# Moving one set of transposes and three load steps in a hand-ordered attention and gated-linear-unit kernel

## The chip, the cores and the metric

The kernel runs on one core of one Trainium2 chip. The metric is device time in microseconds of one execution. Three runs of the kernel before took 190.13 to 190.59 us; their median is 190.49 us.

A core has a matrix engine (PE, TensorE), a vector engine (DVE), a scalar engine (ACT) and a general engine (POOL), each with its own queue of instructions that is worked off in order, and a queue (SP) that issues DMAs and also works in order. An instruction that waits for a semaphore holds up everything behind it in its queue. PE writes into PSUM, which has eight banks here numbered 0 to 7; DVE and ACT read them; POOL and the DMAs work on SBUF alone.

## The reference

There are 8 batches, 8 heads, 576 positions and a head dimension of 64. First comes causal attention with a bias that is a running sum, then a gated linear unit over the 512 columns that the heads make together. Cut to what matters:

```python
scores = scale * np.matmul(q, k.transpose(0, 1, 3, 2))
bias = -(cum[:, :, :, None] - cum[:, :, None, :])        # cum = running sum of max(s, 0)
scores = np.where(causal, -1e9, scores + np.minimum(bias, 0.0))
attn = exp(scores - max); attn = attn / (attn.sum(-1) + 1e-9)
x = np.matmul(attn, v)                                   # heads side by side: (8, 576, 512)

gate_pre = sum over 5 taps of conv_w[k] * x shifted by 4 - k positions
out = (sigmoid(gate_pre) * (x @ w_val)) @ w_out
```

All inputs and the output are float32; the kernel works in bfloat16 between float32 sums.

## The kernel before

**Units of work.** Two heads of one batch are a pair. There are 32 pairs, `n` = 0 to 31, four to a batch: batch `b` = `n // 4`. A step is one small piece of work for one pair, one batch or one tile of output, and is written as a name with its indices, such as `s0.21`. For a batch, K and Q are loaded (`ld_q.b` brings heads 0 to 3 of both Q and K, `ld_k.b` heads 4 to 7 of both, each as two DMAs of 512 KB, line 436), cast to bfloat16 into a buffer `qkb` (`c_q.b`, `c_k.b`, line 374), and transposed on PE: `qq.b.0` transposes what `c_q.b` cast and `qq.b.1` what `c_k.b` cast. Each of the two sets is 32 transposes of half the array (line 630), which alternate between two banks. Each bank is then copied out into `QKT` (`qe.b.p`, `p` = 0 to 3; `qe.b.0` and `qe.b.1` belong to `qq.b.0`, the other two to `qq.b.1`; line 374, a helper that all plain copies share). V is loaded by blocks of 128 positions (`ld_v.b.i`, line 472) and multiplied by a weight on POOL (`vp.b.p`, line 475), which needs all five blocks.

For a pair there are three groups of score products (`s0.n`, `s1.n`, `s2.n`, PE, line 506, each into two banks), their exponentials (`e0.n`, `e1.n`, `e2.n`, ACT, line 557, into one of three buffers P), a causal mask on POOL (`mk.n`, line 580), the product with V (`av0.n` and `av.n` for the two heads, line 595), reciprocal and normalisation on DVE (`rec.n`, `nm.n`, lines 608 and 614) and a transpose back to columns (`xt.n`, line 627, copied by `xe.n`). The convolution has four tap steps (`t1.n` to `t4.n`, on DVE at lines 666 and 671 or on POOL at line 674, some with a product `p2.n` to `p4.n` made ahead on POOL), then a tanh (`th.n`, ACT, line 691), the product with `w_val` (`val`, line 704) and the gate (`glu`, DVE, line 713). Two batches `u` share nine output tiles: `out.u.i` (PE, line 724, four products of 128x512 into one bank), `oe.u.i` (a copy into one of six tiles `ot`) and `st.u.i` (the store, line 732).

**What sets the order.** Nothing is planned when the kernel is built. The table `ORDER` names every step once, and the loop at the end of `main_path` calls the steps in that order. What follows the name is the engine (S for SP, G for POOL, T for PE, A for ACT, V for DVE), then the banks or the buffer: `s0.21:T:0+1:0` puts scores into banks 0 and 1 and their exponentials into P buffer 0. The order of the table is the order of each engine's queue; how the steps of different engines stand to each other is left to the semaphores, which are set by what each step reads and writes. Steps of different engines that only swap places in the table change nothing.

Around the change, the rows of batch 6, the seventh, stand between those of pairs 17 to 20. The banks there are: `qq.6.1` 7 and 3, `qq.6.0` 2 and 5, `out.1.6` 6, `xt.17` 3, `s2.20` 0 and 1, `out.1.8` 2, `av0.19` with `av.19` 6 and 7, `out.1.5` 4, `s0.21` 0 and 1. The scores `s0.20` are in banks 5 and 6, and `xt.18` is in bank 4, where DVE's taps of pair 18 read it. The loop that turns the table into instructions is this:

```python
    for name, e, *slots in steps:                      # line 772
        f, *ix = name.split(".")
        ...
        does[f](engines[e], *ix)                       # line 785
```

The steps that the change touches are written by these functions:

```python
    def qk_T2(e, b, h):                                # qq, line 635
        for p in range(2):
            for j in range(8):
                for r in range(2):
                    half_T(row_bank(b, h, r)[:, p * 512 + j * 64:p * 512 + j * 64 + 64], qk_src(None, b, 2 * h + p, j), r)
```

Of the kernel before, what the change touches and what calls it, by code (L numbers as in the profile page):

```python
# [16 lines left out]
B, H, S, D = 8, 8, 576, 64  # L17
# [229 lines left out]
val.13.0:T:4 t1.16:V:2 e1.18:A s2.18:T:5+6 vp.5.2:G glu.13.0:V val.15.0:T:2 t3.16:V st.1.0:S e2.18:A val.13.1:T:4  # L247
val.15.1:T:0 vp.5.1:G ld_v.6.1:S glu.13.1:V th.15:A:4 t4.16:V s0.19:T:5+6:2 av0.18:T:3+4 e0.19:A vp.5.0:G glu.15.1:V
av.18:T glu.15.0:V ld_v.6.4:S s1.19:T:0+1 rec.18:V s2.19:T:5+6 e1.19:A nm.18:V out.1.4:T:2 vp.5.3:G t2.16:V e2.19:A
tt.6:T:3 ld_v.6.3:S c_q.6:G:0 xt.18:T:4 oe.1.4:V:1 av0.17:T:0+1 te.6:A ld_k.7:S:2 xe.18:V s0.20:T:5+6:1 av.17:T  # L250
t1.18:V:0 e0.20:A qq.6.1:T:7:3 mk.19:G rec.17:V nm.17:V qe.6.3:A mk.20:G out.1.6:T:6 qe.6.2:V ld_v.6.0:S xt.17:T:3
p2.18:G:1 s2.20:T:0+1 qq.6.0:T:2:5 t4.18:V oe.1.6:A:5 qe.6.0:A e2.20:A out.1.8:T:2 qe.6.1:A st.1.6:S xe.17:V c_q.7:G:2
t3.18:V av0.19:T:6+7 th.16:A:1 st.1.2:S av.19:T t1.17:V:1 out.1.5:T:4 rec.19:V t2.18:G nm.19:V oe.1.5:A:3
s0.21:T:0+1:0 t4.17:V e0.21:A s1.20:T:6+7 st.1.5:S xt.19:T:4 ld_v.6.2:S out.1.7:T:5 t2.17:V e1.20:A mk.21:G ld_t.7:S
xe.19:V s1.21:T:0+1 oe.1.8:A:0 s2.21:T:6+7 t3.17:V p3.19:G:0 e1.21:A val.16.0:T:2 t1.19:V:3 val.18.0:T:3 e2.21:A
p4.19:G:1 val.17.0:T:0 glu.16.0:V t2.19:V val.16.1:T:1 th.17:A:0 st.1.4:S s0.22:T:6+7:2 t3.19:G th.18:A:2 glu.17.0:V
# [584 lines left out]
```

## Time and profile before

| what | value |
|---|---|
| median of 3 runs | 190.49 us |
| the profiled execution | 189.88 us |
| its span, first to last instruction | 188.2 us |
| granted TensorE clock, mean | 0.991 |
| PE busy | 173.1 us, 92% of the span |
| ACT busy | 171.5 us, 91% |
| DVE busy | 164.8 us, 88% |
| POOL busy | 162.0 us, 86% |
| DMA, mean over the span | 215 GB/s |

The profiled execution's own time is 1.68 us longer than its span: that lies around the first and the last instruction. All times below are from the start of the span. "Busy" is the sum of the times at which an engine worked on something; since matmuls are pipelined, a busy PE isn't at its peak. A row of a timeline gives the start, the length, the engine, the line in the kernel, the operation with what it writes and reads, and how often it stands there in a row; in brackets stands the idle time of the engine ahead of it, with the engine and line that ended it. Rows that start before the one above has ended overlap, as the engines are pipelined. For DMAs the length is that of the issue on SP; the time until the data has landed is given apart.

### The profile page before, as it was taken

What the parts mean: (1) busy time and instruction counts of PE and PEld (TensorE: products, weight loads), DVE (VectorE), ACT (ScalarE), POOL (GpSimd) and SP (SyncE); (2) the same over time, 40 slices, a digit from 0 to 9 for tenths busy, and PEclk for the clock granted to TensorE, in tenths of its full rate; (3) what the DMA queues carried; (4) which work ended last, traced back from release to release, by engine and by line L of the source; (5) the groups of instructions that cost most, each with busy time, mean ns of one, the idle gap of its engine ahead of it and who ended that gap; (6) DMA issues with size and microseconds to landing.
All of it is one profiled execution on the core that took longest, in us unless ns stands there. A gap on an engine that the chain in (4) does not pass through costs nothing.

```text
span 188.2 us, 6675 instructions
## 1 busy us (share of the span) xinstructions
PE 173.1 (92%) x2719; PEld 114.6 (61%) x2735; DVE 164.8 (88%) x320; ACT 171.5 (91%) x233; POOL 162.0 (86%) x145
## 2 busy tenths in 40 slices
PE   6999797889999999999969997999999999999991
PEld 2557384377757666576846674487566865767660
DVE  4867779879998899998999998889999899999980
ACT  3599969999999989999999988999999999999871
POOL 5149899898999999999999999599989989699530
PEclk9999889999999999999999999999999999999999
DMA  5999999799799999999799998869950003403064
GB/s 181 249 287 279 237 294 206 186 353 325 158 301 351 395 267 232 271 339 252 268 197 250 357 275 254 250 160 259 168 189 4 3 2 115 167 5 115 2 223 174
DMA packets 62283, 40.46 MB, mean 215 GB/s; under 512 B 47333, under 2 KB 49381, under 8 KB 62250
## 3 DMA queue, kind: packets, MB, share of 16 engines
q1 hardware_dynamic: 61706, 39.49, 76.7%
q10 hardware_dynamic: 544, 0.52, 0.8%
q8 instruction: 22, 0.36, 0.8%
q14 instruction: 11, 0.09, 0.1%
HBM read 30.57 MB, written 9.44 MB: 213 GB/s over the span
## 4 chain that ended last, share of the span: by engine, by line
PE 63%; ACT 20%; DMA 5%; SPq 4%; issue 3%; DVE 3%; ACTq 0%; DVEq 0%
PE bank L704 15%; PE bank L724 14%; ACT P L557 13%; PE bank L595 12%; PE bank L506 9%; PE bank L627 4%; PE bank L630 4%; DMA qkf<-in_k_dram 3%; PE bank L621 2%; ACT QKT L374 2%; DMA first<-in_k_dram 2%; SPq L468 1%; PE bank L519 1%; ACT ot L374 1%; ACT th L691 1%
## 5 line engine op out<-in xcount | busy, mean ns | idle before, releaser
L557 ACT ACTIVATE P<-bank 128x1024 bf16<-128x1024 f32 x84 | 83.1, 1044 | 3.3 <-PE bank L506 2.2
L671 DVE SCALAR_TENSOR_TENSOR gp<-bank,cwr,gp 128x574 f32<-128x574 bf16 (+6 forms) x71 | 51.1, 742 | 0.3
L674 POOL TENSOR_TENSOR gp<-gp,pr 128x572 f32<-128x572 f32 (+6 forms) x37 | 46.1, 1250 | 4.8 <-DVE gp L671 2.7
L506 PE MATMUL bank<-QKT 64*128 64x128 bf16 (+4 forms) x592 | 38.2, 237 | 4.6 <-ACT P L557 2.7
L475 POOL TENSOR_TENSOR Vp<-vst,w 128x650 bf16<-128x650 f32 x32 | 40.5, 1288 | 0.2 <-ACT w L395 0.2
L704 PE MATMUL bank<-xT,wv 128*128 128x288 bf16 (+2 forms) x256 | 38.2, 286 | 0.9 <-DVE gp L671 0.5
L595 PEld LDWEIGHTS <-P 128*128 128x128 bf16 x960 | 33.6, 98 | 5.6 <-issue 1.9
L595 PE MATMUL bank<-Vp,P 128*128 128x65 bf16 x960 | 36.5, 194 | 0.4 <-POOL Vp L475 0.2
L724 PE MATMUL bank<-wo,glu 128*128 128x512 bf16 x128 | 34.6, 380 | 2.2 <-ACT QKT L374 1.1
L506 PEld LDWEIGHTS <-QKT 64*128 64x128 bf16 x592 | 19.2, 94 | 22.4 <-issue 16.8
L655 POOL TENSOR_TENSOR pr<-xT,cwr 128x572 f32<-128x572 bf16 (+6 forms) x29 | 29.7, 1031 | 2.0 <-DVE xT L374 0.9
L704 PEld LDWEIGHTS <-wv 128*128 128x128 bf16 x256 | 22.5, 98 | 9.9 <-issue 3.8
L713 DVE SCALAR_TENSOR_TENSOR glu<-th,bank 128x288 bf16<-128x288 f32 (+2 forms) x64 | 26.9, 445 | 1.7 <-ACT th L691 0.5
L580 POOL TENSOR_SCALAR_AFFINE_SELECT P<-P 128x1024 bf16<-128x1024 bf16 (+2 forms) x19 | 19.1, 1010 | 10.0 <-ACT P L557 10.0
L666 DVE SCALAR_TENSOR_TENSOR gp<-xT,cwr,bank 128x576 f32<-128x576 bf16 (+2 forms) x36 | 26.6, 743 | 1.2 <-ACT xT L374 0.2
L614 DVE TENSOR_TENSOR xn<-bank,recs 128x640 bf16<-128x640 f32 (+2 forms) x36 | 26.8, 745 | 0.7
L374 ACT COPY QKT<-bank 128x1024 bf16<-128x1024 bf16 (+1 forms) x21 | 20.9, 1024 | 2.5 <-PE bank L490 1.3
L691 ACT ACTIVATE th<-gp,cwr 128x576 f32<-128x576 f32 x28 | 21.8, 799 | 0.0
L724 PEld LDWEIGHTS <-glu 128*128 128x128 bf16 x144 | 12.3, 97 | 13.5 <-issue 2.8
L374 ACT COPY ot<-bank 128x512 f32<-128x512 f32 x29 | 17.2, 609 | 2.2 <-PE bank L724 2.1
L374 DVE COPY QKT<-bank 128x1024 bf16<-128x1024 bf16 (+1 forms) x15 | 14.5, 969 | 4.1 <-PE bank L630 1.9
L627 PE MATMUL bank<-ident,xn 128*128 128x128 bf16 x164 | 15.0, 220 | 0.9 <-ACT P L557 0.6
(66 smaller groups left out, 183.6 us busy)
## 6 DMA issues: line engine op xcount, KB each, us to landing
out_dram<-ot SPq DMA_DIRECT2D x36, 256.0 KB, 3.1
vst<-in_v_dram SPq DMA_DIRECT2D x28, 256.0 KB, 5.9
first<-in_q_dram SPq DMA_DIRECT2D x6, 512.0 KB, 6.0
first<-in_k_dram SPq DMA_DIRECT2D x6, 512.0 KB, 6.9
qkf<-in_q_dram SPq DMA_DIRECT2D x6, 512.0 KB, 6.4
qkf<-in_k_dram SPq DMA_DIRECT2D x6, 512.0 KB, 6.4
vst<-in_v_dram SPq DMA_DIRECT2D x15, 128.0 KB, 4.6
first<-in_q_dram SPq DMA_DIRECT2D x4, 256.0 KB, 4.0
```

The lines of the kernel that those rows point to most:

```text
L374: (act.copy if e is act else e.tensor_copy)(dst, src)
L475: e.tensor_tensor(Vps[b % 2][:, :, HP[p]], vslot(b)[:, :, HP[p]], w[:, :, b * 8 + 2 * p:b * 8 + 2 * p + 2].unsqueeze(3).to_broadcast([128, ...
L506: pe.matmul(ps[:, hh, c0:c0 + nq], QKTs[b % 2][r, 1, p, k0:k0 + 128], QKTs[b % 2][r, 0, p, q0:q0 + nq], **kw)
L557: act.activation(out=Pt(n)[:, :, step * 512:(step + 1) * 512], in_=pair((f"s{step}", n)), func=AF.Exp, scale=0.125)
L595: pe.matmul(ps[:, o:o + 65], lhsT, Vps[b % 2][:, kb, 2 * p + w, :], start=(kb == 0), stop=(kb == qb))
L614: vec.tensor_tensor(xns[b % 2][:, g, p * 128:(p + 1) * 128].rearrange("t g (w d) -> t w g d", w=2), ps[:, :, :, 0:64], recs[:, n, :, g].un ...
L655: pool.tensor_tensor(pr, xTs[b % 2][:, c, 4 + lo - m:4 + hi - m], r.to_broadcast([128, hi - lo]), ALU.mult)
L671: vec.scalar_tensor_tensor(gp[:, lo:hi], xps(n, *h)[:, lo - m:hi - m], r, gp[:, lo:hi], ALU.mult, ALU.add)
L674: pool.tensor_tensor(gp[:, lo:hi], gp[:, lo:hi], prs[at[f"p{m}", n, *h][0]][:, lo:hi], ALU.add)
L704: pe.matmul(ps, wv[:, dc, c * 128:(c + 1) * 128], xTs[b % 2][:, dc, 4 + lo:4 + hi], start=(dc == 0), stop=(dc == 3))
L713: vec.scalar_tensor_tensor(glu2[:, c, o + lo:o + hi], th[:, lo:hi], 1.0, ps, ALU.add, ALU.mult)
L724: pe.matmul(bank_of(u, i), glu2[:, c, i * 128:i * 128 + 128], wo[:, c, :], start=(c == 0), stop=(c == 3))
```

## The change

The same steps are called, on the same engines, with the same banks and buffers. In the table, `qq.6.0` moves up to stand behind `qq.6.1`; `e2.20` moves down behind `th.16`; and `ld_v.6.3`, `ld_k.7` and `ld_v.6.0` move down behind the stores `st.1.6` and `st.1.2`. Two of the lines of the table that are new (the second begins with the moved loads):

```diff
+qq.6.1:T:7:3 mk.19:G rec.17:V nm.17:V qq.6.0:T:2:5 qe.6.3:A mk.20:G out.1.6:T:6 qe.6.2:V qe.6.0:A xt.17:T:3 p2.18:G:1
+ld_v.6.3:S ld_k.7:S:2 ld_v.6.0:S av.19:T t1.17:V:1 e2.20:A out.1.5:T:4 rec.19:V t2.18:G nm.19:V oe.1.5:A:3
```

On PE, where `qq.6.1` (which reads `qkb1`) ends, the rows stand like this; + is the kernel after, - the kernel before, and a row names the semaphores it waits for by their engine:

```order
 L630 LDWEIGHTS qkb1_103
 L630 MATMUL bank_153<-ident_67,qkb1_103 128x64
-L724 LDWEIGHTS glu2_115
-L724 MATMUL bank_153<-wo_143,glu2_115 128x512 [waits Activation_49]
+L630 LDWEIGHTS qkb0_102 [waits Pool_49]
+L630 MATMUL bank_153<-ident_67,qkb0_102 128x64 [waits DVE_49]
+L630 LDWEIGHTS qkb0_102
+L630 MATMUL bank_153<-ident_67,qkb0_102 128x64 [waits Activation_49]
```

The first product of `out.1.6`, which waited for ACT there, now follows the 32 transposes of `qq.6.0` (which read `qkb0`); these stood behind `s2.20` before. On ACT, in the same place, with the copies of `qe.6` into `QKT0`, of `oe.1.6` into `ot5` and of `oe.1.5` into `ot3`, the exponentials `e0.20` and `e2.20` into `P1`, and the tanh `th.16` into `th1`:

```order
 L557 ACTIVATE P1_117<-bank_153 128x2x512
-L374 COPY QKT0_107<-bank_153 128x2x2x256
-L374 COPY ot5_133<-bank_153 128x512
-L374 COPY QKT0_107<-bank_153 128x2x2x256
-L557 ACTIVATE P1_117<-bank_153 128x2x512
+L374 COPY QKT0_107<-bank_153 128x2x2x256 x2
+L374 COPY ot5_133<-bank_153 128x512
 L374 COPY QKT0_107<-bank_153 128x2x2x256
 L691 ACTIVATE th1_124<-gp2_121,cwr_144 128x576
+L557 ACTIVATE P1_117<-bank_153 128x2x512
 L374 COPY ot3_131<-bank_153 128x512
```

`qe.6.3` and `qe.6.0` now stand together ahead of `oe.1.6`, and `e2.20` stands behind `qe.6.1` and `th.16`. On SP, with `ld_v` into `vst0`, the two DMAs of `ld_k.7` into `qkf0`, and the stores from `ot5` (`st.1.6`), `ot4` (`st.1.2`) and `ot3` (`st.1.5`):

```order
 L472 DMA vst0_92<-in_v_dram 64x8x64
+L732 DMA out_0_dram<-ot5_133 128x512
+L732 DMA out_0_dram<-ot4_132 128x512
 L472 DMA vst0_92<-in_v_dram 128x8x64
 L436 DMA qkf0_136<-in_q_dram 64x4x512
 L436 DMA qkf0_136<-in_k_dram 64x4x512
 L472 DMA vst0_92<-in_v_dram 128x8x64
-L732 DMA out_0_dram<-ot5_133 128x512
-L732 DMA out_0_dram<-ot4_132 128x512
 L732 DMA out_0_dram<-ot3_131 128x512
```

Four DMAs, the three load steps, now stand behind two stores, the first of which waits for `oe.1.6`. On DVE and POOL the order is the same in both kernels.

More of the change, by code (lines that the diff above doesn't have):

```diff
@@ L249 @@
 av.18:T glu.15.0:V ld_v.6.4:S s1.19:T:0+1 rec.18:V s2.19:T:5+6 e1.19:A nm.18:V out.1.4:T:2 vp.5.3:G t2.16:V e2.19:A
[L250 to L253, printed above, removed]
+tt.6:T:3 c_q.6:G:0 xt.18:T:4 oe.1.4:V:1 av0.17:T:0+1 te.6:A xe.18:V s0.20:T:5+6:1 av.17:T t1.18:V:0 e0.20:A
+qq.6.1:T:7:3 mk.19:G rec.17:V nm.17:V qq.6.0:T:2:5 qe.6.3:A mk.20:G out.1.6:T:6 qe.6.2:V qe.6.0:A xt.17:T:3 p2.18:G:1
+s2.20:T:0+1 t4.18:V oe.1.6:A:5 out.1.8:T:2 qe.6.1:A st.1.6:S xe.17:V c_q.7:G:2 t3.18:V av0.19:T:6+7 th.16:A:1 st.1.2:S
+ld_v.6.3:S ld_k.7:S:2 ld_v.6.0:S av.19:T t1.17:V:1 e2.20:A out.1.5:T:4 rec.19:V t2.18:G nm.19:V oe.1.5:A:3
 s0.21:T:0+1:0 t4.17:V e0.21:A s1.20:T:6+7 st.1.5:S xt.19:T:4 ld_v.6.2:S out.1.7:T:5 t2.17:V e1.20:A mk.21:G ld_t.7:S
```

## The prediction

> **What bounds the kernel now.** I read the page first. Its chain of the work that ended last is shared out by engine like this:
>
> ```profile
> PE 63%; ACT 20%; DMA 5%; SPq 4%; issue 3%; DVE 3%; ACTq 0%; DVEq 0%
> ```
>
> No single engine bounds the program: the end passes from PE to ACT and back. So I took the chain in order of time at the place of the change, between 112 and 120 us (start, length, what):
>
> ```profile
> 115.19 1.01 ACT QKT L374
> 116.24 1.02 PE bank L724 x4
> ```
>
> The first is `qe.6.0`, ACT's copy of the transposes out of PSUM; the second is `out.1.8`, a product that goes into the bank which that copy empties. The chain runs through the steps that the change moves, so time won or lost here counts. Next, PE alone in order of time (start, length, engine, line, what; in brackets its idle time before and who ended it):
>
> ```profile
> 112.14 0.64 PE L630 MATMUL bank<-ident,qkb 64*128 64x64 bf16 x32
> 112.82 1.02 PE L724 MATMUL bank<-wo,glu 128*128 128x512 bf16 x3
> 113.92 0.44 PE L627 MATMUL bank<-ident,xn 128*128 128x128 bf16 x5
> 114.29 0.39 PE L506 MATMUL bank<-QKT 64*128 64x320 bf16 x4
> 114.52 0.63 PE L630 MATMUL bank<-ident,qkb 64*128 64x64 bf16 x32
> 116.24 1.02 PE L724 MATMUL bank<-wo,glu 128*128 128x512 bf16 x4 [1.10 <-ACT QKT L374]
> 117.10 1.08 PE L595 MATMUL bank<-Vp,P 128*128 128x65 bf16 x30
> 118.02 1.03 PE L724 MATMUL bank<-wo,glu 128*128 128x512 bf16 x3
> 118.98 0.83 PE L506 MATMUL bank<-QKT 64*128 64x128 bf16 x12
> ```
>
> These are, in order, `qq.6.1`, `out.1.6`, `xt.17`, `s2.20`, `qq.6.0`, `out.1.8`, `av0.19` with `av.19`, `out.1.5`, and `s0.21` with `s1.20`. PE stands still for 1.10 us ahead of `out.1.8`. ACT in the same stretch:
>
> ```profile
> 111.75 1.02 ACT L557 ACTIVATE P<-bank 128x1024 bf16<-128x1024 f32 x1 [0.34 <-PE bank L506]
> 112.85 1.01 ACT L374 COPY QKT<-bank 128x1024 bf16<-128x1024 bf16 x1
> 113.88 0.59 ACT L374 COPY ot<-bank 128x512 f32<-128x512 f32 x1
> 115.18 1.01 ACT L374 COPY QKT<-bank 128x1024 bf16<-128x1024 bf16 x1 [0.71 <-PE bank L630]
> 116.09 1.03 ACT L557 ACTIVATE P<-bank 128x1024 bf16<-128x1024 f32 x1
> 117.00 1.02 ACT L374 COPY QKT<-bank 128x1024 bf16<-128x1024 bf16 x1
> 117.90 0.80 ACT L691 ACTIVATE th<-gp,cwr 128x576 f32<-128x576 f32 x1
> 119.08 0.58 ACT L374 COPY ot<-bank 128x512 f32<-128x512 f32 x1 [0.39 <-PE bank L724]
> 119.56 1.95 ACT L557 ACTIVATE P<-bank 128x1024 bf16<-128x1024 f32 x2
> ```
>
> These are `e0.20`, `qe.6.3`, `oe.1.6`, `qe.6.0`, `e2.20`, `qe.6.1`, `th.16`, `oe.1.5`, then `e0.21` and `e1.20`. ACT waits 0.71 us for `qq.6.0` and then 0.39 us for `out.1.5`, which is late because PE stood still for ACT: one loss, paid on both engines. Its small gap ahead of `oe.1.6` (113.88 against 112.85 + 0.91, the step from one full-width start to the next at 115.18 and 116.09) is 0.12. All of ACT's loss is therefore 0.71 + 0.39 + 0.12 = 1.22 us.
>
> **The change on PE and ACT.** Nothing is added or removed; instructions only change places. `qq.6.0` now follows `qq.6.1`. What it waits for: its data, cast on POOL by `c_q.6` (first row below), done at 110.08 + 1.89 = 111.97; bank 5, which `e0.20` empties at 112.77; bank 2, emptied earlier on DVE. POOL, with rows that are needed later:
>
> ```profile
> 110.08 1.89 POOL L374 CAST qkb<-first 128x2048 bf16<-128x2048 f32 x1
> ...
> 120.67 1.09 POOL L580 TENSOR_SCALAR_AFFINE_SELECT P<-P 128x1024 bf16<-128x1024 bf16 x1 [2.29 <-ACT P L557]
> ...
> 125.48 1.89 POOL L374 CAST qkb<-qkf 128x2048 bf16<-128x2048 f32 x1
> 127.33 1.40 POOL L674 TENSOR_TENSOR gp<-gp,pr 128x572 f32<-128x572 f32 x1
> ```
>
> So `qq.6.0` starts at 112.82, where `out.1.6` starts now after the same wait for `e0.20`. It delays what follows by about 0.57 us (0.63 less the overlap that pipelined matmuls have). PE then runs `out.1.6` at 113.39, `xt.17` about 0.9 later at 114.29, `s2.20` at 114.66 (113.92 to 114.29 is 0.37), and reaches `out.1.8` at 114.9 (114.29 to 114.52 is 0.23).
>
> ACT: `e0.20` and `qe.6.3` stay where they are. `qe.6.0` follows at 112.85 + 0.91 = 113.76; its transposes end by 113.45, so it doesn't wait, and it ends at 114.77, before PE asks for bank 2 at 114.9. The 1.10 us is gone. Then `oe.1.6` at 114.67 (`out.1.6` ended near 114.4), `qe.6.1` 0.48 later (119.08 to 119.56) at 115.15, `th.16` 0.90 later at 116.05, and `e2.20`, now behind these, at 116.73 (0.80 less 0.12 of overlap, as 117.00 + 1.02 against 117.90). It ends at 117.75, where it ends at 117.12 now. That is the one price on this path: `s0.21` needs banks 0 and 1 from `e2.20`.
>
> What is late next on PE: `av0.19` comes at 114.9 + 0.86 = 115.76; its bank 6 is free when `oe.1.6` ends, 115.26. `out.1.5` comes 0.92 later, at 116.68, and needs bank 4 from DVE's `t3.18`, the first of these rows:
>
> ```profile
> 115.53 0.80 DVE L671 SCALAR_TENSOR_TENSOR gp<-bank,cwr,gp 128x573 f32<-128x573 bf16 x1
> 116.25 0.80 DVE L666 SCALAR_TENSOR_TENSOR gp<-xT,cwr,bank 128x576 f32<-128x576 bf16 x1
> 118.29 0.22 DVE L608 RECIPROCAL recs<-bank 128x10 f32<-128x10 f32 x1 [1.24 <-PE bank L595]
> ```
>
> It ends at 116.33: in time by 0.35. `out.1.5` ends at about 117.7, and `s0.21` starts at 117.8 behind `e2.20` (118.98 now: 1.18 earlier). `oe.1.5` starts at about 117.8 (119.08 now), and `e0.21` near 118.3 (119.56 now): 1.2 to 1.3 earlier. DVE's `rec.19` waits 1.24 now; its predecessor ends at 117.05, so it too can come 1.24 earlier. POOL's `mk.21` waits 2.29 for `e0.21`, so POOL can follow with 1.1 to spare. I take 1.2, the loss of ACT taken away whole. The ends: 1.3 by the starts just worked out; 0.7 if neighbours on ACT don't overlap (five steps at about 0.1 more each).
>
> **Whether it lasts to the end.** After 119 the engines look like this (stretch, its length, then busy time of PE, PEld, DVE, ACT and POOL; clock; DMA share; GB/s):
>
> ```profile
> 114.00:119.00 5.00, 3.85 (x80) 2.60 (x82) 3.73 (x7) 3.98 (x5) 4.38 (x4) 1.00 1.01 321
> 119.00:147.00 28.00, 27.11 (x442) 18.47 (x444) 26.69 (x49) 27.58 (x35) 25.52 (x21) 1.00 0.60 155
> ```
>
> ACT is busy for 27.58 of 28 us, and all four are chained to each other. If all can start 1.2 earlier, all stay 1.2 earlier; only what doesn't move with them can take it back. That is the loads.
>
> **The change on SP.** The stores `st.1.6` and `st.1.2` now stand ahead of `ld_v.6.3`, `ld_k.7` (two DMAs) and `ld_v.6.0`. `st.1.6` waits for `oe.1.6`, so these four DMAs wait with it. SP now (the third row is `ld_v.6.0`, the fourth begins with `st.1.6`):
>
> ```profile
> 110.20 2.51 SPq L436 DMA_DIRECT2D qkf<-in_q_dram  x1
> 112.75 0.62 SPq L436 DMA_DIRECT2D qkf<-in_k_dram  x1
> 113.42 0.60 SPq L472 DMA_DIRECT2D vst<-in_v_dram  x1
> 114.49 5.53 SPq L732 DMA_DIRECT2D out_dram<-ot  x3
> ```
>
> After: `st.1.6` at 115.3, where `oe.1.6` ends, and then some 0.6 each: `st.1.2` 115.9, `ld_v.6.3` 116.5, `ld_k.7` 117.0 and 117.6, `ld_v.6.0` 118.2. The second half of `ld_k.7` is issued 4.9 us later than now. Time to landing of the K and Q loads between 100 and 135 us, and of the V load ahead of `ld_k.7`:
>
> ```profile
> DMA to landing us min/median/max: 5.4/6.4/7.5
> vst<-in_v_dram SPq DMA_DIRECT2D x1, 256.0 KB, 6.8
> ```
>
> So it lands between 117.6 + 5.4 = 123.0 and 117.6 + 7.5 = 125.1. By bytes: the two stores, `ld_v.6.3` and `ld_k.7` are 1.84 MB; at the 321 GB/s of the row above that is 5.7 us, with some 2 us ahead of the first arrival 123.0. Who waits: `c_k.7` on POOL, at 125.48 now and wanted at 124.28; behind it `t4.19` (127.33, to 128.73), and for that ACT's `th.19`:
>
> ```profile
> 129.37 0.78 ACT L691 ACTIVATE th<-gp,cwr 128x576 f32<-128x576 f32 x1
> ```
>
> `th.19` starts 0.64 after `t4.19` ends, so `c_k.7` may start as late as 124.9 at no cost. The middle of the landing range, 124.0, is hidden; its late end, 125.1, would cost 0.2. The V loads have `vp.6.2` behind `t4.19`, later still, and I cost them at nothing.
>
> The V load of 256 KB takes 6.8 us where K and Q loads of 512 KB take 6.4, so bytes alone don't tell when what stands behind a V load lands, and I keep the whole landing range. By the Trainium skill, DMA: Bandwidth & Descriptors, Specifications, a transfer needs pieces of at least 512 B for line rate; a V row here is 64 floats, 256 B, and the trace agrees. By the same section's ceiling of 435 GB/s the 1.84 MB would take 4.2 us, an estimate by which `ld_k.7` would land 1.5 us sooner and the sum would stay as it is.
>
> **The sum.** The profiled execution took 189.88 us, 0.61 under the median of the runs, 190.49. 189.88 - 1.2 = 188.7; on the scale of the median, 189.3. About 0.3% (0.57 us) is what a measurement of this kernel can tell from no change.
>
> **The rivals.**
> - *The gain is smaller* (0.7): ACT's neighbours don't overlap. 189.8. Against it: starts 0.91 apart at 115.18, 116.09 and 117.00.
> - *The K load takes the gain back.* For no change `c_k.7` would have to start at 124.9 + 1.2 = 126.1, 8.5 us after its issue. Beyond the longest landing above, but reached if the issue stalls for a second as at 110.20 (2.51 us). About 190.5.
> - *Slower, by the same load.* It decides from a landing of 126.7 on. With the stall of 110.20 whole (1.9 more) and the longest landing it comes at 117.6 + 1.9 + 7.5 = 127.0; then `t4.19` ends at 130.3 and `th.19` starts 1.0 later than now: 191.5. For it: the landing and the stall were both seen. Against it: after the change SP issues nothing between the load ahead of `st.1.6` and 115.3, so what was queued has time to drain.
> - *PE's clock falls.* Granted clock in 114 to 119 is 1.00, with 32 transposes and a pause of 1.10 in it. If it halved for 2 of these 5 us, 1.5 us of work would take 3: 189.3 + 1.5 = 190.8. By the Trainium skill, TensorE: Matmul & The Clock Gate, Part 4, transposes don't count as busy for the gate in the same way, and 64 now stand together; the trace shows no fall after 32.
>
> **How the numbers follow.** Forecast 0.60 (own range 188.9 to 189.7), smaller gain 0.10, taken back 0.15, slower by the load 0.13, clock 0.02. Faster is 0.60 + 0.10 = 0.70; same 0.15; slower 0.13 + 0.02 = 0.15. The range leaves out the two slower cases and a little of the forecast's low end: 188.8 to 190.8.
>
> **What would show it.** Right: 64 transposes in one piece from 112.8 to about 113.4; no idle time on PE ahead of `out.1.8`; `qe.6.3` and `qe.6.0` back to back; `e0.21` near 118.3; POOL's `c_k.7` near 124.3 with no wait for a DMA; the rest of the trace as now, 1.2 earlier. Wrong: idle time on POOL ahead of `c_k.7` that a DMA ends, and then on ACT ahead of `th.19`; or `s0.21` held up by `e2.20` past 118.5.

## The result and the profile after

The kernel after takes 188.82 us (median of 11 runs) against 190.49 us (median of 11 runs of the kernel before): a ratio of 0.9916, 95% interval 0.9891 to 0.9941. That is 1.67 us, with an interval of about 1.1 to 2.1 us. The profiled execution took 188.30 us, with a span of 186.5 us (188.2 before). The forecast was 189.3. How much of the difference lies at the place of the change, the traces tell.

The chain that ended last, by engine; before, PE's share was 63% and ACT's 20%, and DMA had 5% and SP's queue 4%. These shares change from execution to execution (a second one of the kernel after has PE 59%, ACT 14% and SP's queue 12%), so nothing below rests on them:

```profile
PE 72%; ACT 18%; DVE 4%; issue 3%; POOL 0%; ACTq 0%; POOLq 0%; DVEq 0%
```

PE in order of time, at the place of the change:

```profile
111.75 1.30 PE L630 MATMUL bank<-ident,qkb 64*128 64x64 bf16 x64
112.98 1.04 PE L724 MATMUL bank<-wo,glu 128*128 128x512 bf16 x4
113.86 0.44 PE L627 MATMUL bank<-ident,xn 128*128 128x128 bf16 x5
114.23 0.39 PE L506 MATMUL bank<-QKT 64*128 64x320 bf16 x4
114.56 1.04 PE L724 MATMUL bank<-wo,glu 128*128 128x512 bf16 x4
115.43 1.08 PE L595 MATMUL bank<-Vp,P 128*128 128x65 bf16 x30
116.34 1.03 PE L724 MATMUL bank<-wo,glu 128*128 128x512 bf16 x4
117.42 0.72 PE L506 MATMUL bank<-QKT 64*128 64x128 bf16 x12
```

The 64 transposes are one piece, and `out.1.8` (114.56) follows `s2.20` with no idle time, where 1.10 us stood before. ACT in the same stretch:

```profile
111.35 1.02 ACT L557 ACTIVATE P<-bank 128x1024 bf16<-128x1024 f32 x1 [0.34 <-PE bank L506]
112.45 1.93 ACT L374 COPY QKT<-bank 128x1024 bf16<-128x1024 bf16 x2
114.27 0.61 ACT L374 COPY ot<-bank 128x512 f32<-128x512 f32 x1
114.74 1.05 ACT L374 COPY QKT<-bank 128x1024 bf16<-128x1024 bf16 x1
115.65 0.81 ACT L691 ACTIVATE th<-gp,cwr 128x576 f32<-128x576 f32 x1
116.32 1.04 ACT L557 ACTIVATE P<-bank 128x1024 bf16<-128x1024 f32 x1
117.41 0.58 ACT L374 COPY ot<-bank 128x512 f32<-128x512 f32 x1
117.89 1.95 ACT L557 ACTIVATE P<-bank 128x1024 bf16<-128x1024 f32 x2
```

The idle times of 0.71 and 0.39 us are gone. `e0.20` (first row) starts at 111.35 and `e0.21` (last row) at 117.89: 6.54 us apart, against 111.75 and 119.56, 7.81, before. So the place of the change gives 1.27 us. The other 0.40 us of the two profiled executions lies ahead of `e0.20`, where the two programs are the same on every engine but SP.

From `e0.21` to the end of the span it is 188.2 - 119.56 = 68.64 us before and 186.5 - 117.89 = 68.61 after: nothing of the 1.27 is given back, as far as spans read to 0.1 us can tell. The moved loads on SP, then POOL, then the tanh `th.19` on ACT:

```profile
114.90 1.41 SPq L732 DMA_DIRECT2D out_dram<-ot  x2
116.36 0.43 SPq L472 DMA_DIRECT2D vst<-in_v_dram  x1
116.83 0.71 SPq L436 DMA_DIRECT2D qkf<-in_q_dram  x1
117.59 0.61 SPq L436 DMA_DIRECT2D qkf<-in_k_dram  x1
118.25 0.60 SPq L472 DMA_DIRECT2D vst<-in_v_dram  x1
```

```profile
118.99 1.09 POOL L580 TENSOR_SCALAR_AFFINE_SELECT P<-P 128x1024 bf16<-128x1024 bf16 x1 [1.01 <-ACT P L557]
...
124.04 1.89 POOL L374 CAST qkb<-qkf 128x2048 bf16<-128x2048 f32 x1 [0.18 <-DMA qkf<-in_k_dram]
125.89 1.40 POOL L674 TENSOR_TENSOR gp<-gp,pr 128x572 f32<-128x572 f32 x1
```

```profile
127.69 0.78 ACT L691 ACTIVATE th<-gp,cwr 128x576 f32<-128x576 f32 x1
```

POOL's cast `c_k.7` does wait for the K load, by 0.18 us. `t4.19` ends at 127.29 and `th.19` starts at 127.69, so the wait costs nothing, but the cover left (the time by which `t4.19` could still come later at no cost) is 0.40 us.

### The profile page after: what moved, and what is told of

Read it like the earlier page. It is cut to its first block, busy times and chain, and to the rows that moved or that the text cites. A ratio compares the mean times of both kernels' runs of the same rounds, so it can differ in the third digit from the quotient of the medians.

```text
span 186.5 us, 6691 instructions
## 1 busy us (share of the span) xinstructions
PE 173.7 (93%) x2735; PEld 114.3 (61%) x2735; DVE 165.3 (89%) x320; ACT 171.3 (92%) x233; POOL 162.1 (87%) x145
## 4 chain that ended last, share of the span: by engine, by line
PE 72%; ACT 18%; DVE 4%; issue 3%; POOL 0%; ACTq 0%; POOLq 0%; DVEq 0%
PE bank L704 15%; PE bank L724 15%; PE bank L595 13%; ACT P L557 13%; PE bank L506 11%; PE bank L621 6%; PE bank L627 4%; PE bank L630 3%; PE bank L490 2%; PE bank L519 1%; PE bank L481 1%; ACT ot L374 1%; DVE gp L666 1%; DVE gp L671 1%; ACT th L691 1%
## 5 line engine op out<-in xcount | busy, mean ns | idle before, releaser
L506 PE MATMUL bank<-QKT 64*128 64x128 bf16 (+4 forms) x592 | 38.1, 237 | 4.5 <-ACT P L557 2.5
L724 PE MATMUL bank<-wo,glu 128*128 128x512 bf16 x144 | 36.0, 380 | 0.0
L506 PEld LDWEIGHTS <-QKT 64*128 64x128 bf16 x592 | 19.3, 94 | 22.1 <-issue 16.4
```

Of the source, the lines that this page charges most:

```text
L506: pe.matmul(ps[:, hh, c0:c0 + nq], QKTs[b % 2][r, 1, p, k0:k0 + 128], QKTs[b % 2][r, 0, p, q0:q0 + nq], **kw)
L724: pe.matmul(bank_of(u, i), glu2[:, c, i * 128:i * 128 + 128], wo[:, c, :], start=(c == 0), stop=(c == 3))
```

## The experiments

Two intervals sort the executions. The first, from the start of `e0.20` to that of `e0.21` on ACT, is the place of the change; the second, from the start of `e0.21` to the end of the span, is the rest. The first two columns of the table are read off ACT's timeline of each profiled execution, and the others follow from them and the span. The ratio is the measured time against the kernel before on the same chip, with its 95% interval; it isn't the quotient of the two medians and can differ from it by 0.001. Only "between" and "rest" tell where time was won; each is read from one execution.

| kernel | e0.20 | e0.21 | between | rest | ratio |
|---|---|---|---|---|---|
| before | 111.75 | 119.56 | 7.81 | 68.64 | 1 |
| after | 111.35 | 117.89 | 6.54 | 68.61 | 0.9916 (0.9891 to 0.9941) |
| after, again | 112.36 | 119.11 | 6.75 | 68.59 | 0.9925 (0.9899 to 0.9951) |
| order on PE and ACT only | 112.37 | 118.91 | 6.54 | 68.59 | 0.9927 (0.9896 to 0.9957) |
| loads only | 112.62 | 120.43 | 7.81 | 68.67 | 1.0011 (0.9990 to 1.0033) |
| half way | 113.28 | 120.37 | 7.09 | 68.63 | 0.9967 (0.9943 to 0.9991) |
| exponential back | 111.87 | 118.46 | 6.59 | 68.64 | 0.9946 (0.9928 to 0.9964) |
| K load one later | 112.53 | 119.07 | 6.54 | 69.63 | 0.9961 (0.9936 to 0.9987) |
| K load much later | 111.68 | 118.22 | 6.54 | 70.38 | 1.0149 (1.0111 to 1.0186) |

**The changed kernel again**, without an edit.

> The changed kernel itself, once more beside the others. Theory (one stall taken off PE and ACT, 1.27 us by the two profiles between e0.20 and e0.21): e0.21 starts 6.5 us after e0.20 (before: 7.8), ratio about 0.992 to 0.994. The 0.40 us by which its first profile was already ahead at e0.20, where the two programs are still the same, is jitter: it should come out differently here.

The gain is 1.17 us by the medians (188.96 against 190.13) and 1.4 by the ratio, 0.9925. `e0.20` now comes at 112.36, later than in the trace of before: the 0.40 us ahead of it was jitter (a difference between executions that no edit makes), as expected. Over all traced executions here `e0.20` starts between 111.35 and 113.28, though the programs are the same up to 110 us on every engine but SP. "Between" is 0.21 longer than in the first execution: ACT's `oe.1.5` waited for PE. On PE the delay arises in `xt.17`, which took 0.66 us instead of 0.44; the trace names no cause.

```profile
118.63 0.58 ACT L374 COPY ot<-bank 128x512 f32<-128x512 f32 x1 [0.25 <-PE bank L595]
```

**The order on PE and ACT only.** Against the kernel after, on SP:

```diff
+ld_v.6.3:S
+ld_k.7:S:2
+ld_v.6.0:S
 st.1.6:S
 st.1.2:S
-ld_v.6.3:S
-ld_k.7:S:2
-ld_v.6.0:S
```

> Only the order on PE and ACT is changed; the three load steps stand where they stood before. Theory: the whole gain is in this part, e0.21 starts 6.5 us after e0.20 and the ratio is that of the full change within 0.002, or better by at most 0.001, since POOL's cast of the moved K load waited 0.18 us for its DMA in the full change and this was hidden. Rival (the loads moved behind the stores give a part of the gain, since the DMA engines are clear for the stores): slower than the full change by 0.002 or more.

188.98 us, ratio 0.9927; 6.54 us between. The whole gain is in this part. The rival, that the moved loads give a part of the gain, asked for a ratio worse by 0.002 or more, and it isn't. POOL's cast starts without a wait:

```profile
124.83 1.89 POOL L374 CAST qkb<-qkf 128x2048 bf16<-128x2048 f32 x1
```

**The loads only.** The three steps are moved as in the diff above with + and - exchanged, now against the kernel before.

> Only the three load steps are moved behind the two stores; PE and ACT keep the order of before. st.1.6 is then issued near 114.5 and the second half of the K load near 117; it lands near 123.4, when POOL wants it at 125.5. Theory: no change, ratio 0.998 to 1.002, e0.21 7.8 us after e0.20, no DMA wait ahead of POOL's cast. Rival (the loads give a part of the gain): ratio under 0.997.

190.39 against 190.13 us, ratio 1.0011 with 1 in its interval; 7.81 us between. PE and ACT wait as before, here PE ahead of `out.1.8`:

```profile
117.11 1.02 PE L724 MATMUL bank<-wo,glu 128*128 128x512 bf16 x4 [1.10 <-ACT QKT L374]
```

So the loads by themselves give nothing.

**Half way.** Against the kernel before, on PE; ACT and SP keep their order:

```diff
 qq.6.1:T:7:3
 out.1.6:T:6
+qq.6.0:T:2:5
 xt.17:T:3
 s2.20:T:0+1
-qq.6.0:T:2:5
 out.1.8:T:2
```

> Only the 32 transposes of qq.6.0 are moved, and only half the way: behind out.1.6, ahead of xt.17. ACT and SP keep their order. Theory by the starts of the trace: qq.6.0 ends near 114.4 instead of 115.15, so ACT's qe.6.0 follows oe.1.6 with no wait (0.71 won); PE still waits for qe.6.0 ahead of out.1.8, by about 0.5 instead of 1.10. e0.21 starts 7.0 us after e0.20, a gain of about 0.8 us, ratio 0.995 to 0.997. Rival (only the order of the copies on ACT matters): no change, since ACT's order is that of before.

189.74 us, ratio 0.9967; 7.09 us between, a gain of 0.72 where 0.8 was expected. ACT's copy `qe.6.0` no longer waits for the transposes, and PE's wait for the copy is cut to 0.39:

```profile
115.41 0.59 ACT L374 COPY ot<-bank 128x512 f32<-128x512 f32 x1
115.98 1.01 ACT L374 COPY QKT<-bank 128x1024 bf16<-128x1024 bf16 x1
```

```profile
117.05 1.02 PE L724 MATMUL bank<-wo,glu 128*128 128x512 bf16 x4 [0.39 <-ACT QKT L374]
```

So 0.72 of the 1.27 us comes from the place of the transposes on PE, with ACT's order as it was; the rival, that only the order on ACT matters, is out. PE still waits, as `qe.6.0` starts at 115.98, right behind `oe.1.6` and just after the transposes end at 115.95. The other 0.55 came only with the last step up on PE and ACT's new order together: no run parts these two.

**The exponential put back.** Against the kernel after, on ACT:

```diff
 qe.6.0:A
 oe.1.6:A:5
+e2.20:A
 qe.6.1:A
 th.16:A:1
-e2.20:A
 oe.1.5:A:3
```

> The changed kernel with the exponential e2.20 put back ahead of qe.6.1 and th.16, all else as changed. s0.21 is then free of e2.20 about 1.5 us sooner. Theory: ACT is full from e0.20 to e0.21 either way, so e0.21 keeps its start, 6.5 us after e0.20, within 0.15, and the time is that of the changed kernel within 0.002. Rival (e2.20 moved down is what won the time): e0.21 comes 0.5 us or more later than in the changed kernel.

188.87 us (188.96 and 188.82 for the kernel after), ratio 0.9946 against a median of before of 189.82 on this chip; 6.59 us between. `e2.20` stands here right behind `oe.1.6`, and `e0.21` comes no sooner:

```profile
115.51 1.02 ACT L557 ACTIVATE P<-bank 128x1024 bf16<-128x1024 f32 x1
...
118.46 1.96 ACT L557 ACTIVATE P<-bank 128x1024 bf16<-128x1024 f32 x2
```

The place of `e2.20` is neither the gain nor a price that the runs can tell: in this trace and in the first of the kernel after, ACT shows no idle time from `e0.20` to `e0.21`.

**The K load one DMA later.** Against the kernel after, on SP:

```diff
 ld_v.6.3:S
-ld_k.7:S:2
 ld_v.6.0:S
+ld_k.7:S:2
 st.1.5:S
```

> The changed kernel with both halves of ld_k.7 moved behind one more DMA only, the V load ld_v.6.0. Second half issued near 118.2 instead of 117.6, so that it lands 0.6 to 1.5 us later. In the changed kernel th.19 has 0.4 us of slack. Theory: th.19 starts 0.2 to 1.1 us later, ratio to before 0.994 to 0.999. Rival (there is cover left): as the changed kernel, 0.9925.

189.44 us, ratio 0.9961: about half of the gain is gone by the ratios, though their intervals overlap (0.9936 to 0.9987 here, 0.9899 to 0.9951 for the kernel after). The trace, of the longest of the twelve executions (190.46 us), shows where. POOL's cast, then ACT's `th.19`:

```profile
126.66 1.89 POOL L374 CAST qkb<-qkf 128x2048 bf16<-128x2048 f32 x1 [1.61 <-DMA qkf<-in_k_dram]
```

```profile
129.93 0.78 ACT L691 ACTIVATE th<-gp,cwr 128x576 f32<-128x576 f32 x1 [0.94 <-POOL gp L674]
```

`th.19` starts 10.86 us after `e0.21` instead of 9.80, and the rest is longer by as much, 69.63 against 68.61. In this execution SP issued the second half at 119.53, 0.46 us after `e0.21`; in the kernel after it did so 0.30 us ahead of `e0.21`. The load then took 7.0 us to land, where POOL's cast in the kernel after started 6.45 us after the issue: 0.76 us of the delay is the issue, and the rest the landing.

**The K load much later.** Against the kernel after, on SP:

```diff
 ld_v.6.3:S
-ld_k.7:S:2
 ld_v.6.0:S
 st.1.5:S
 ld_v.6.2:S
+ld_k.7:S:2
 ld_t.7:S
```

> The changed kernel with both halves of ld_k.7 moved two DMAs further down, behind st.1.5 and ld_v.6.2. Its second half is then issued near 119.8 (117.6 in the changed kernel), lands near 126.2, and POOL's cast starts near 126.3 instead of 124.0. Theory (the slack of th.19 behind t4.19 is 0.4 in the changed kernel's trace, and from there on ACT pays): th.19 starts 1.6 to 2.0 us later than in the changed kernel, the whole gain is lost, ratio to before 0.998 to 1.004. Rival (the load has cover to spare, or later stages take the delay up): the ratio stays at 0.993 or less.

Three DMAs, counting `ld_v.6.0`, now stand ahead of the load that stood behind them. The profiled execution is as expected. POOL's cast, and `th.19`:

```profile
126.47 1.89 POOL L374 CAST qkb<-qkf 128x2048 bf16<-128x2048 f32 x1 [2.28 <-PE bank L506]
```

```profile
129.75 0.78 ACT L691 ACTIVATE th<-gp,cwr 128x576 f32<-128x576 f32 x1 [1.60 <-POOL gp L674]
```

The releaser named in the first row had long been done; the cast waits for the K load, issued at 119.98 with 6.3 us to landing, which is 126.28. `th.19` comes 11.53 us after `e0.21` instead of 9.80, 1.73 later, and this execution took 190.29 us, a ratio of 1.0025. But the median of the six runs is 192.42 us, ratio 1.0149, which is over the expected 1.004: the other five took 191.75 to 193.36, and without the two longest the median is still 191.85. So four more executions of the same kernel were traced, numbered 2 to 5 here.

> The kernel with the late K load once more, to see what its slower executions are made of: its profiled execution lost 1.8 us behind e0.21, but its other runs were 1.5 to 3 us above that one. Theory (the time to landing differs from run to run, and past the slack each us of it is a us of the end): the K load lands later than 6.3 us after its issue whenever the span is longer than 188.6, POOL's cast and th.19 come later by as much, and span minus the start of th.19 stays at 58.8 within 0.3. Rival (the loss lies in a later stage, such as the loads behind the K load): span minus the start of th.19 grows.

> As for the second look at the late K load: one more execution, for the spread.

> The late K load once more, in search of one of its executions of 191.7 us and more, of which none is in a trace so far. Theory: as in the looks before, span minus the start of th.19 is 58.8 within 0.3, and what is longer lies between the issue of the K load and th.19. Rival: it lies before e0.20 or behind th.19.

> As for the fourth look at the late K load: one more execution, in search of a slower one; span minus the start of th.19 is 58.8 within 0.3.

Executions 2, 3 and 4 took 190.96, 190.64 and 191.08 us (the kernel before beside them: 190.13 in the median for 2 and 3, one run of 190.98 for 4 and 5), and span minus the start of `th.19` was 58.76, 58.83 and 58.83, as in the kernels before (58.83) and after (58.81). The expectation that a longer span goes with a longer landing didn't hold in execution 2: its load landed 6.2 us after the issue, no later than the 6.3 of the first, and its span was 0.6 us longer mainly because `e0.20` came 0.54 us later. Execution 5 is one of the long ones: 193.26 us. Its `th.19`, then PE behind it:

```profile
131.36 0.77 ACT L691 ACTIVATE th<-gp,cwr 128x576 f32<-128x576 f32 x1 [2.65 <-POOL gp L674]
```

```profile
132.67 0.39 PE L506 MATMUL bank<-QKT 64*128 64x64 bf16 x4 [2.47 <-DVE glu L713]
```

Two things add up. `th.19` comes 12.57 us after `e0.21`, 1.04 more than in the first execution: SP issued the second half of the load 2.46 us after `e0.21` (1.76 there), and it took 6.7 us to land (6.3 there). And span minus the start of `th.19` is 191.6 - 131.36 = 60.24, 1.4 more than anywhere else. The granted clock of PE (the third number from the end; 1.00 is full speed) fell there, by stretches of 2 us:

```profile
132.00:134.00 2.00, 1.17 (x9) 0.45 (x11) 1.83 (x4) 2.00 (x4) 2.00 (x3) 1.00 0.65 149
134.00:136.00 2.00, 2.00 (x39) 1.36 (x39) 2.00 (x4) 1.84 (x3) 2.00 (x2) 0.52 0.89 198
136.00:138.00 2.00, 2.00 (x27) 1.18 (x26) 1.69 (x3) 1.68 (x4) 2.00 (x3) 0.62 0.06 15
```

After PE had stood for 2.47 us its clock read 0.52 and 0.62 over these 4 us, which is 3.4 us at half. In execution 4, where PE stood for 1.62 us at the same place, it stayed at 1.00:

```profile
131.78 0.39 PE L506 MATMUL bank<-QKT 64*128 64x64 bf16 x4 [1.62 <-DVE glu L713]
```

```profile
134.00:136.00 2.00, 2.00 (x52) 1.48 (x45) 2.00 (x4) 2.00 (x4) 2.00 (x2) 1.00 0.45 96
```

The expectation for executions 4 and 5, that all of the extra time lies ahead of `th.19`, fell with execution 5: behind it lie 1.4 us, where the clock fell. That the idle time of PE made it fall is inferred from this one execution, and another fall warns against a simple rule: in seven of the thirteen traces the clock goes to 0.50 for 3.4 us near 22 us, in execution 5 too, and there no idle time of PE was over 0.63 us in the 8 us before. PE was merely thinly used, busy for 1.16 of 2 us:

```profile
20.00:22.00 2.00, 1.16 (x13) 0.70 (x13) 1.82 (x4) 2.00 (x5) 2.00 (x3) 0.86 0.87 200
22.00:24.00 2.00, 1.97 (x27) 0.85 (x28) 0.65 (x1) 2.00 (x3) 2.00 (x2) 0.50 0.96 263
```

The same program shows this early fall in executions 1 and 5 and not in 2, 3 and 4. That the other long executions are made like execution 5 isn't shown, since none of them is in a trace.

## Why the prediction was right

The time predicted was 189.3 us, with 188.9 to 189.7 as the forecast's own range, and 188.82 and 188.96 were measured. The direction and the mechanism held. The first median is 0.08 us below that own range and only 0.02 above the low end of the whole range, 188.8 to 190.8; that it stayed inside is luck, since its size holds some 0.4 us that the change didn't make.

- *The stall and its size.* "The loss of ACT taken away whole", 1.2 us, measured 1.27 between `e0.20` and `e0.21` (1.06 in the second execution). The rival of a smaller gain, 0.7, is out: the two copies in a row took 1.93 us, where one alone takes 1.01, so neighbours on ACT do overlap. The starts worked out on PE and ACT, shifted by the 0.40 us by which the execution was ahead, hold within 0.07 us: `out.1.8` worked out at 114.5 and measured at 114.56; `th.16` 115.65 and 115.65; `e2.20` 116.33 and 116.32; `e0.21` 117.9 and 117.89. What is late next on PE was named rightly too: bank 4 and bank 6 were free in time, and `s0.21` (117.42) follows the end of `e2.20` (117.36).
- *It lasts to the end.* The rest is 68.59 to 68.67 us in the seven executions of the table in which the K load was in time, that of before among them. Everything behind `e0.21` moved as one.
- *The loads.* The landing of `ld_k.7` was put at 123.0 to 125.1 and taken at the middle, 124.0, with no wait at the cast. What was off is the issue, not the landing: SP issued the second half at 117.59, which is 118.0 on the scale of the prediction and not 117.6, and the cast started 6.45 us later, near the median of 6.4 that was used. So the cast came 0.4 later than worked out, and it waited 0.18 us for the load, and 0.33 in the second execution. This is the one sign that came out wrong; the cover that was worked out for it took it up, with 0.40 us left, and 0.25 in the second execution. The K load one DMA later shows how near the edge it stood: there the rival "the K load takes the gain back" is half true. That the load held is therefore in part luck.
- *The rival on the clock.* In the changed kernel the clock stays at 1.00 with 64 transposes together, so they didn't lower it. Where it fell behind the change, in execution 5 of the late load, an idle time of PE stood ahead of the fall. By the Trainium skill, TensorE: Matmul & The Clock Gate, Part 1, the clock falls to half after an idle window of about 3.4 us. Execution 5 agrees on the half (0.52), but its idle time was shorter, 2.47 us, and the falls near 22 us came with none over 0.63.
- *The size of the median.* 1.67 us in the first comparison and 1.17 in the second. The traces explain 1.27 and 1.06 by the change; the first comparison's surplus is inside its interval, and its profiled execution had 0.40 of it ahead of the change.

## What to carry to other kernels

Where two engines each wait for the other within a microsecond, look for one work item that both waits share: moving 32 transposes up by three places, with the copy that follows them moved up on ACT, took away waits of 0.71 and 0.39 us on ACT and 1.10 us on PE, which were one loss of 1.27; the transposes moved up by two places alone gave 0.72. Before a load is moved down, follow its data to the first instruction that has no slack; here that was the third step behind the load, it had 0.64 us before and 0.40 and 0.25 after, and one more DMA in front cost 0.5 us by the medians and 1.0 in the one trace, of a long execution. To tell a small gain from the jitter of the start, measure between two instructions on either side of the change in each trace, and from there to the end.

## What the runs showed of the hardware

- The start of a step deep in the program, `e0.20`, moves by up to 1.9 us from one execution to another (111.35 to 113.28), while the rest from `e0.21` repeats within 0.08 us in the seven whose K load came in time (their spans are read to 0.1 us). In these traces what spread of the total remains, beside the change and the late loads, lies in the first 112 us. The early fall of the clock doesn't account for it: `e0.20` starts at 111.68 to 112.62 in the seven executions with it and at 111.35 to 113.28 in the six without.
- An idle time of 2.47 us on PE was followed by 3.4 us at half the clock, in an execution that lost 1.4 us there; 1.62 us of idle time at the same place cost no clock. A late load can so cost more than its lateness. The clock also fell near 22 us in seven traces without an idle time over 0.63 us, so the length of one idle time doesn't settle it. Each of these eight falls lasted 3.4 us.
- A wait for a DMA can carry another engine's name: the same wait of POOL's cast reads "PE bank L506" in the first execution of the late K load and "DMA qkf<-in_k_dram" in execution 2 of the same kernel. The time of issue and of landing told which it was.
